# A spectral kernel of two heads: small column repairs given to another engine, the first loads put into one queue, a hint for the last branch, and a new order of the steps

## The chip, the core and the metric

The kernel runs on one core of a Trainium2 chip. Its engines are TensorE (PE, whose weight loads the profile lists apart as PEld), VectorE (DVE), ScalarE (ACT), GpSimd (POOL) and SyncE (SP). Each runs its own instructions in order; semaphores tie them together. SP issues nearly all loads, POOL the stores and a few small loads. The metric is the device time of one execution in microseconds, the median of several runs.

## What is computed

Two independent heads, joined along the last axis. Head A is a global filter: a real 2-D Fourier transform of a 2048 x 512 array, a product with a complex filter, and the transform back. Head B is Fourier mixing with the DFT matrices given as inputs.

```python
X = rfft2(A_x)                       # 1 x 2048 x 257, complex
a = irfft2(X * (A_w_r + 1j * A_w_i), s=(2048, 512))
h_re = einsum("bsd,ed->bse", B_x, dft_hid_re)
h_im = einsum("bsd,ed->bse", B_x, dft_hid_im)
b = einsum("ts,bse->bte", dft_seq_re, h_re) - einsum("ts,bse->bte", dft_seq_im, h_im)
return concatenate([a, b], axis=-1)
```

All data are float32. The two sequence matrices have 2048 x 2048 numbers each, 32 MB together.

## The kernel before, in words

The kernel does not multiply by the large matrices. It computes both heads by fast transforms, with tables of cosines and sines, and compares the given DFT matrices with those tables element by element. At the end one number, `flag`, says whether all compared equal. If they did not, a general path (`_b_from_c`, behind `tc.If` in L814) computes head B by plain products. With these inputs the general path is jumped over.

All work is cut into named steps, and `PLAN` (L23 to L39) is a list of their names. The loop at L808 runs through it and emits the instructions of each step, so the list sets the order in which PE, DVE, ACT and SP see them. POOL's instructions follow the same list. The steps:

- **Head A, forward.** `xa` loads a tile of x. `fold` (DVE, L344 to L353) adds and subtracts its mirrored halves. `hid` (PE, L360 to L365) transforms the hidden axis, `zs` (ACT, L369) copies the result from PSUM, `f16` (PE, L376) does a length-16 transform along the sequence, and `ys` (ACT, L380) scatters it into the large buffer `fz`. There are eight of `hid` to `ys` and five folds (0, 1, 3, 5, 7).
- **Head A, spectrum**, in eight slots n = 0 to 7 (slot 2 has a special form). `w` loads the filter and the table `fi`. `tr` (PE, L422) transposes, `ez` (ACT, L426) copies one half, `sf` (DVE, L432 to L434) combines mirrored halves, `fwd` (PE, L441) finishes the sequence transform, `prod` (DVE, L472 to L476) and `comb` (DVE, L480 to L484) multiply by the complex filter, `inv` (PE, L502) starts the way back, and `ev` (ACT, L509) writes into `fz`. In slot 2, `sx`, `g` and `spec` stand in for `sf`. Column 0 of the first half is an exception to the general formulas (two real spectra are packed into it). It is repaired by small operations of four numbers per partition: L434 in `sf`, L472 in `prod` (it puts a prepared filter column from `we` into `w`), and L484 in `comb` (a product with `sgn`).
- **Head A, inverse.** `hi` (PE, L537), `eu` (ACT, L542), `g16` (PE, L549), `sc` (ACT, L553), `eo` (DVE, L558) and the stores `st` (POOL) run eight times over the hidden axis and the length-16 transform. `hi` reads all of `fz`, so it starts after the last `ev`.
- **Head B.** `xb` loads, `xr` (ACT) reverses, `al` (PE, L629 and L630) and `av` (ACT) do the first transform in 16 pieces; `bh` (PE, L651 to L655), `hv` (ACT), `ro` (PE, L667), `y1` and `y3` (ACT), `y2` (DVE, L682) and the stores `pt` (POOL) do the rest in eight.
- **The comparison.** `cl` loads 1 MB of the given matrices, `cc` (DVE, L724) compares it with the table that `tt` loaded. There are 34 such pairs. `sg` (ACT) changes the sign of half a table in place. `rs`, `pf` and `flag` reduce the result.

`blk` is a ring of six buffers that the x tiles of both heads and the blocks of the comparison share; a load waits until the step that read the buffer's earlier content is done. The tiles named `pa` (three, two banks each) and `pb` (two, one bank each) are PSUM.

At the start ACT issues the first table `ta` (L298), SP the x tiles, and POOL the tile `eye`, the corner values `wsp`, `odd` and `turn`. Nine dummy products (L311) keep PE busy. `late` reloads `ta` with the tables of the inverse stage.

Of the kernel before, what the change touches and what calls it, by code (L numbers as in the profile page):

```python
# [24 lines left out]
ys0 xb2 fold5 f16_1 zs2 xb3 f16_2 ys1 xb1 hid3 ys2 cl3 cc1 hid4 zs3 fold7 cl4 f16_3 zs4 f16_4 ys3 hid5 ys4 cl5
cl6 cc2 hid6 zs5 w0 f16_5 zs6 cl7 xr0 hid7 ys5 w1 cc3 al0 zs7 f16_6 av0 cc4 sg0 f16_7 ys6 w2 cc5 al1 ys7 late
al2 av1 cc6 tr0 av2 tr1 ez0 tr2 sf0 ez1 al3 sf1 fwd0 xb4 av3 cc7 xb7 ez2 xb6 xb5 fwd1 xb8 cl8 prod0 sg1 tr3
xb9 xb10 comb0 fwd2 cl9 xb11 xb12 prod1 xb13 xr1 xb14 g2 al4 comb1 ez3 inv0 av4 cl10 sx2 al5 w3 ev0 al6 sf3
av5 spec2 al7 cc8 av6 w4 inv1 av7 xr2 prod2 tr4 xb15 ev1 al8 ez4 cc9 al9 av8 cl11 al10 av9 sf4 w5 al11 av10
comb2 fwd3 av11 cl12 cl14 xr3 cl13 fwd4 cc10 spy al12 al13 prod3 av12 al14 av13 al15 cc11 av14 w6 inv2 cl15  # L30
av15 cl16 cc12 tt2 cl17 comb3 bh8 cl19 ev2 bh0 hv8 prod4 inv3 hv0 comb4 tr5 w7 ev3 tr6 ez5 cc13 ro0 ez6 cc14
inv4 y10 bh1 ev4 y20 cl18 cl20 sf5 y30 rx sf6 tr7 hv1 ry bh2 cc15 ez7 pt0 ro1 hv2 cc16 tt3 fwd5 y11 cl21 ro2
y21 cl23 sg2 fwd6 sf7 y12 y31 y22 bh3 pt1 prod5 y32 fwd7 hv3 pt2 comb5 bh4 prod6 ro3 hv4 inv5 y13 comb6 ro4
ev5 y23 inv6 y14 prod7 y33 bh5 pt3 ev6 y24 comb7 y34 bh6 hv5 pt4 ro5 hv6 cc17 inv7 y15 bh7 ev7 y25 cl22 tt4
cc18 y35 ro6 hv7 pt5 hi0 y16 cc19 cc20 cl24 cl25 hi1 eu0 cc21 cl26 g16_0 y26 eu1 cl27 cc22 sg3 hi2 sc0 y36
cc23 pt6 hi3 eo0 eu2 cl28 cl29 cc24 g16_1 cc25 cl32 ro7 eu3 cc26 cl30 g16_2 y17 sc1 sg4 hi4 eo1 cl31 sc2 y27
st0 eo2 y37 pt7 hi5 cc27 eu4 cc28 cl33 g16_3 cc29 hi6 sc3 eu5 cc30 g16_4 eo3 cc31 g16_5 st1 eu6 sc4 hi7 sc5
eo4 eo5 cc32 st2 g16_6 eu7 cc33 g16_7 sc6 sc7 eo6 eo7 st30 rs st31 pf flag
# [893 lines left out]
```

## Time and profile before

| | |
|---|---|
| median of 3 runs | 192.7 us (192.49 to 192.76) |
| the profiled execution | 192.64 us, of which 190.3 us are the span from the first to the last instruction |
| moved by DMA | 66.05 MB, 346 GB/s over the span |
| granted TensorE clock | 0.983 |
| q1 (loads issued by SP) | 56.33 MB, 75.3% of the 16 DMA engines |
| q0 (POOL's stores and loads) | 9.08 MB, 12.3% |

The page's second part cuts the span into 40 slices of 4.76 us and gives the busy share of each in tenths. DVE and ACT read so:

```profile
DVE  1499999579899999999999999999999989779940
ACT  2015768699524493523444252354325273322300
```

A row of the groups reads: line, engine, operation, written tile <- read tiles, shape, count | busy us in all, mean ns of one | idle time of the engine just before these instructions, and what ended it. The costliest are the comparison and the first product of the inverse stage:

```profile
L724 DVE SCALAR_TENSOR_TENSOR blk<-blk,odd,tt 128x2048 f32<-128x2048 f32 x16 | 37.3, 2348 | 0.6 <-DMA blk<-in_cm 0.3
L537 PE MATMUL pa<-ta,fz 128*128 128x256 f32 x128 | 29.6, 388 | 0.0
```

A float32 product appears as more than one record, so counts of PE rows are twice those of the program. The view of one line lists operations as count: shortest/median/longest in ns, first and last start in us; a "q" behind an engine's name is its sequencer. In the view of waits a row names who waited for whom, the total in us, how often, and the longest.

### The profile page before, as it was taken

The page shows a single profiled execution, that of the slowest core. Times are in us where ns is not written, and L with a number is a line of the kernel's source. Part 1 is how long each engine was busy: PE and PEld are TensorE (multiplying, and loading weights), DVE is VectorE, ACT ScalarE, POOL GpSimd, SP SyncE. Part 2 cuts the span into 40 slices and gives each one's busy share as a digit, 9 for nine tenths or more (in the row PEclk, how much of TensorE's full clock was granted, in tenths as well). Part 3 has the DMA queues.
Part 4 walks back from the last instruction along what each step waited for, and adds up shares of the span by engine and source line. Part 5 has one row for each costly group of instructions (what it writes and reads, how often), then busy time and mean ns, then how long its engine had stood idle before and what let it go on. Part 6 is the DMA issues. An engine that isn't in the chain of part 4 may idle for free.

```text
span 190.3 us, 2768 instructions
## 1 busy us (share of the span) xinstructions
PE 169.9 (89%) x1017; PEld 147.1 (77%) x1017; DVE 166.3 (87%) x240; ACT 83.9 (44%) x114; POOL 23.6 (12%) x33
## 2 busy tenths in 40 slices
...
DVE  1499999579899999999999999999999989779940
ACT  2015768699524493523444252354325273322300
...
DMA  6979999999999999999999989234889999996551
GB/s 188 416 310 432 418 436 398 419 413 416 409 403 418 412 406 326 400 418 309 366 416 409 410 307 418 101 115 124 308 357 419 424 414 420 421 412 230 223 173 63
DMA packets 19619, 66.05 MB, mean 347 GB/s; under 512 B 1776, under 2 KB 2672, under 8 KB 18704
## 3 DMA queue, kind: packets, MB, share of 16 engines
q1 hardware_dynamic: 16784, 56.33, 75.3%
q0 software_dynamic: 2672, 9.08, 12.3%
q10 hardware_dynamic: 144, 0.39, 0.7%
q8 instruction: 10, 0.16, 0.3%
...
HBM read 57.41 MB, written 8.39 MB: 346 GB/s over the span
## 4 chain that ended last, share of the span: by engine, by line
DVE 52%; DMA 35%; issue 7%; SPq 1%; POOL 1%; DVEq 0%; POOLq 0%
DMA blk<-in_cm 27%; DVE blk L724 24%; DVE work L476 7%; DMA tt<-tab_hs 5%; DMA wsp_sb<-in_wsp 3%; DVE work L558 3%; DVE work L482 2%; DVE work L480 2%; DVE work L483 2%; DVE work L481 2%; DVE yb L682 2%; DVE work L433 2%; DVE work L432 2%; DVE work L344 1%; DVE work L682 1%
## 5 line engine op out<-in xcount | busy, mean ns | idle before, releaser
L724 DVE SCALAR_TENSOR_TENSOR blk<-blk,tt 128x2048 f32<-128x2048 f32 (+2 forms) x24 | 41.4, 1755 | 5.8 <-DMA blk<-in_cm 5.8
L724 DVE SCALAR_TENSOR_TENSOR blk<-blk,odd,tt 128x2048 f32<-128x2048 f32 x16 | 37.3, 2348 | 0.6 <-DMA blk<-in_cm 0.3
L537 PE MATMUL pa<-ta,fz 128*128 128x256 f32 x128 | 29.6, 388 | 0.0
L537 PEld LDWEIGHTS pa<-ta,fz 128*128 128x128 f32 x128 | 28.8, 305 | 0.4 <-issue 0.2
L542 ACT COPY work<-pa 128x1024 f32<-128x1024 f32 x8 | 8.1, 1014 | 20.7 <-PE pa L537 12.5
L476 DVE TENSOR_TENSOR work<-pa,w 128x1024 f32<-128x1024 f32 x14 | 16.5, 1220 | 0.6
L502 PEld LDWEIGHTS pa<-fi,work 128*128 128x128 f32 x112 | 13.4, 192 | 4.5 <-DVE work L484 2.6
L549 PEld LDWEIGHTS pa<-ta,work 128*128 128x128 f32 x128 | 15.3, 192 | 1.8 <-PE pa L549 1.2
L549 PE MATMUL pa<-ta,work 128*128 128x128 f32 x128 | 15.5, 275 | 1.0 <-DVE work L558 1.0
L380 ACT COPY fz<-pa 128x1024 f32<-128x1024 f32 x8 | 15.3, 1976 | 2.4 <-PE pa L376 2.4
L502 PE MATMUL pa<-fi,work 128*128 128x128 f32 x112 | 13.8, 276 | 2.4 <-DVE work L484 1.8
L376 PE MATMUL pa<-ta,work 128*128 128x128 f32 x128 | 15.1, 275 | 0.0
L369 ACT COPY work<-pa 128x1024 f32<-128x1024 f32 x8 | 8.1, 1013 | 15.8 <-PE pa L365 15.7
L376 PEld LDWEIGHTS pa<-ta,work 128*128 128x128 f32 x128 | 14.7, 192 | 0.0
L629 PE MATMUL pb<-fb,blk 128*128 128x200 f32 (+1 forms) x64 | 14.6, 309 | 0.0
L630 PE MATMUL pb<-fb,xr 128*128 128x200 f32 (+1 forms) x64 | 14.6, 309 | 0.0
L441 PE MATMUL pa<-work,fi 128*128 128x512 f32 x28 | 13.1, 595 | 1.4 <-DMA fi<-tab_fi 1.4
L509 ACT COPY fz<-pa 128x1024 f32<-128x1024 f32 x8 | 8.1, 1013 | 11.0 <-PE pa L502 7.9
L629 PEld LDWEIGHTS pb<-fb,blk 128*128 128x128 f32 x64 | 10.8, 190 | 0.5 <-issue 0.5
L558 DVE TENSOR_TENSOR work<-pa,work 128x512 f32<-128x512 f32 x16 | 10.1, 683 | 0.8 <-ACT work L553 0.8
L630 PEld LDWEIGHTS pb<-fb,xr 128*128 128x128 f32 x64 | 10.8, 190 | 0.0
L441 PEld LDWEIGHTS pa<-work,fi 128*128 128x128 f32 x28 | 5.1, 190 | 7.1 <-issue 6.8
...
## 6 DMA issues: line engine op xcount, KB each, us to landing
blk<-in_cm SPq DMA_DIRECT2D x32, 1024.0 KB, 12.3
...
```

The costliest lines, as they stand in the source:

```text
L369: act.copy(zs, flat(at["pd", i]))
L376: mm(y[:, r, c], zs[:, r, 128 * c : 128 * c + 128], f16, start=True, stop=True)
L380: act.copy(fz.rearrange("p c k (n g) -> p g (c k n)", g=16)[:, i::8], flat(at["py", i]))
L441: mm(flat(px[:, h]), ft[:, 0], flat(t[:, h]), start=True, stop=True)
L476: TT(out=m[:, h].rearrange("p i (r q) f -> p i r (q f)", r=2), in0=x2, in1=w2, op=MUL)
L502: mm(pi[:, i, q], lhs[i], it[:, 0], start=True, stop=True)
L537: mm(pu[:, k, h], gz[:, 2 * h + q, 2 * j + k], at["di"][:, h, q], start=q == 0, stop=q == 1)
L549: mm(po[:, k, q // 2, q % 2], u[:, k, q], at["g16"], start=True, stop=True)
L558: TT(out=ob[:, r, :, 2 * half : 2 * half + 2].rearrange("p k j s -> p j k s"), in0=at["po", j][:, :, 0], in1=sc, op=op)
L629: mm(bank[:, lo : lo + w], x[:, g, k], fb[:, n // 15, 0, :w], start=True, stop=False)
L630: mm(bank[:, lo : lo + w], xr[:, g, k], fb[:, n // 15, 1, :w], start=False, stop=True)
L724: dve.scalar_tensor_tensor(raw, raw, k, v, op0=MUL, op1=ALU.not_equal, accum_out=stat[:, i : i + 1])
```

## The change

- The repairs of column 0 leave DVE. L434 becomes the step `tf`, L472 the step `wf`, L484 the step `yf`, all on ACT; `yf` is a copy and a multiplication by -1 in place of one product with `sgn`, which goes away.
- The first table's 641 hidden-axis columns are loaded by SP, as the step `ta` behind `xa0`. The length-16 table moves into a tile `square` beside `eye`, loaded by POOL. `late` now loads 1024 columns into `ta` and, in a second load, the table of `g16` over the first half of `square`.
- `we` comes after `fold1`. There are 14 dummy products where there were 9.
- Twelve steps before the end, a branch hint is placed on PE, ACT and DVE for the branch over the general path, with a barrier for the step order that makes no engine wait.
- `PLAN` is a new list.

```diff
-xa0 xa1 xa2 xa3 tt0 cl0 xa5 xa7 we fb fold0 cl1 fold1 tt1 hid0 bt fold3 cl2 hid1 zs0 f16_0 zs1 cc0 xb0 hid2
+xa0 ta tt0 xa1 xa2 xa3 xa5 cl0 fb fold0 cl1 hid0 bt xa7 fold1 tt1 we hid1 zs0 cl2 fold3 f16_0 zs1 f16_1 ys0
...
-    tf = const("ta", 1152)[:, :769]
-    act.dma_start(tf, tabs["first"][:, :769])
-    eye = const("eye", P, src=tabs["first"][:, 769:], by=pool)
+    tf = const("ta", 1024)[:, :641]
+    square = const("square", 2, P, src=tabs["first"][:, 641:].rearrange("p (i f) -> p i f", i=2), by=pool)
+    f16, eye = square[:, 0], square[:, 1]
+    @step("ta")
+    def _():
+        load(tf, tabs["first"][:, :641])
...
-    for _ in range(9):
+    for _ in range(14):
...
-                dve.tensor_copy(t[:, 0, :, :, 0], pz[:, :, 0, :, 0])
+            @step(f"tf{n}")
+            def _():
+                act.copy(t[:, 0, :, :, 0], at["pz", n][:, :, 0, :, 0])
...
+        @step(f"wf{n}")
+        def _():
+            act.copy(at["w", n][:, 0, :, :, 0], we[:, e].rearrange("p f r -> p r f"))
...
-            dve.tensor_copy(w[:, 0, :, :, 0], we[:, e].rearrange("p f r -> p r f"))
...
-            TT(out=yo[:, 0, :, :, 0], in0=y[:, 0, :, :, 0], in1=sgn, op=MUL)
+        @step(f"yf{n}")
+        def _():
+            act.copy(yo[:, 0, 0, :, 0], y[:, 0, 0, :, 0])
+            act.mul(yo[:, 0, 1, :, 0], y[:, 0, 1, :, 0], -1.0)
...
-        tl = const("ta", 1152, src=tabs["late"], by=pool)
-        at["g16"] = tl[:, 1024:]
+        tl = const("ta", 1024, src=tabs["late"][:, :1024], by=pool)
+        pool.dma_start(f16, tabs["late"][:, 1024:])
...
-    for name in PLAN.split():
+    plan = PLAN.split()
+    for at_step, name in enumerate(plan):
+        if at_step == len(plan) - 12:
+            tc.no_sync_barrier()
+            tc.mark_branch_hint_location("general", hint="LikelyTaken", engines=[e.engine for e in (pe, act, dve)])
         steps.pop(name)()
...
-    with tc.If(small == 0):
+    with tc.If(small == 0, label="general"):
```

The list moves steps in many places; three of them matter below. The first is on DVE, where the spectral stage begins. Before the change, the rows of `sf0`, `sf1`, `cc7`, `prod0` and `comb0` (`pa` is PSUM, `blk` a block of the comparison, `work` the working buffer):

```order
L432 TENSOR_TENSOR work<-pa,work 128x2x256
L433 TENSOR_TENSOR work<-work,pa 128x2x256
L434 COPY work<-pa 128x4
L432 TENSOR_TENSOR work<-pa,work 128x2x256
L433 TENSOR_TENSOR work<-work,pa 128x2x256
L434 COPY work<-pa 128x4
L724 SCALAR_TENSOR_TENSOR blk,stat<-blk,tt 128x2048
L472 COPY w<-we 128x4
L476 TENSOR_TENSOR work<-pa,w 128x1024 x2
```

DVE's rows of the change at the same place (lines are 3 to 13 higher there):

```order
L435 TENSOR_TENSOR work<-pa,work 128x2x256
L436 TENSOR_TENSOR work<-work,pa 128x2x256
L435 TENSOR_TENSOR work<-pa,work 128x2x256
L436 TENSOR_TENSOR work<-work,pa 128x2x256
L485 TENSOR_TENSOR work<-pa,w 128x1024 x2
L489 TENSOR_TENSOR work<-work 128x2x2x128
L490 TENSOR_TENSOR work<-work 128x2x256
L491 TENSOR_TENSOR work<-work 128x2x256
L492 TENSOR_TENSOR work<-work 128x2x256
L737 SCALAR_TENSOR_TENSOR blk,stat<-blk,tt 128x2048
```

The small copies are gone, and the comparison `cc7` has moved from ahead of `prod0` to behind `comb0`.

The second place is ACT's, at the same point of the change: `ez0`, `wf0`, `ez1`, `av2`, `tf0`, `wf1`, `av3`, `tf1`, `wf2`, `ez2` and `yf0` in this order (`yall` is head B's buffer):

```order
L429 COPY work<-pa 128x512
L477 COPY w<-we 128x4
L429 COPY work<-pa 128x512
L647 COPY yall<-pb 128x43x8
L440 COPY work<-pa 128x4
L477 COPY w<-we 128x4
L647 COPY yall<-pb 128x43x8
L440 COPY work<-pa 128x4
L477 COPY w<-we 128x4
L429 COPY work<-pa 128x1024
L496 COPY work<-work 128x2
L497 ACTIVATE work<-work 128x2
```

The rows of L440, L477, L496 and L497 are new on this engine; each stands in line with copies that wait for PE.

The third place is the end on DVE. Before, the last two comparisons, the last two `eo` (four rows) and the reduction:

```order
L724 SCALAR_TENSOR_TENSOR blk,stat<-blk,odd,tt 128x2048
L724 SCALAR_TENSOR_TENSOR blk,stat<-blk,tt 128x2048
L558 TENSOR_TENSOR work<-pa,work 128x2x2x128 x4
L798 TENSOR_REDUCE rs<-stat 128x1
L806 TENSOR_SCALAR flag<-pb 128x1
```

The same place of the change on DVE, with the hint:

```order
L737 SCALAR_TENSOR_TENSOR blk,stat<-blk,odd,tt 128x2048
L942 BRANCH_PREFETCH_HINT
L571 TENSOR_TENSOR work<-pa,work 128x2x2x128 x4
L737 SCALAR_TENSOR_TENSOR blk,stat<-blk,tt 128x2048
L811 TENSOR_REDUCE rs<-stat 128x1
L819 TENSOR_SCALAR flag<-pb 128x1
```

The last comparison has moved behind the last `eo`, so the last stores can leave before it.

More of the change, by code (lines that the diff above doesn't have):

```diff
@@ L23 @@
 PLAN = """
-xa0 xa1 xa2 xa3 tt0 cl0 xa5 xa7 we fb fold0 cl1 fold1 tt1 hid0 bt fold3 cl2 hid1 zs0 f16_0 zs1 cc0 xb0 hid2
[L25 to L38, printed above, removed]
+xa0 ta tt0 xa1 xa2 xa3 xa5 cl0 fb fold0 cl1 hid0 bt xa7 fold1 tt1 we hid1 zs0 cl2 fold3 f16_0 zs1 f16_1 ys0
@@ new lines @@
+fold5 xb0 xb3 xb2 hid3 ys1 hid2 zs3 cc0 cl3 f16_3 zs2 cc1 cl4 f16_2 ys3 hid5 ys2 xb1 fold7 hid4 zs5 cl5 f16_5
+zs4 cl6 cc2 hid6 ys5 w0 xb4 f16_4 hid7 cc3 ys4 zs6 zs7 f16_6 w1 cc4 xr0 f16_7 sg0 w2 cc5 al0 ys6 late ys7 al1
+av0 tr0 cc6 av1 tr1 ez0 wf0 al2 ez1 sf0 al3 av2 sf1 tf0 wf1 fwd0 cl7 av3 xb7 tf1 xb6 xb5 tr2 prod0 xb8 wf2
+xb10 fwd1 ez2 cl9 cl8 comb0 fwd2 xb11 cc7 yf0 xb9 xb12 inv0 g2 xr1 prod1 w3 sg1 al4 ev0 sx2 al5 w4 av4 tr3
+comb1 av5 spec2 al6 ez3 al7 av6 sf3 yf1 tr4 cl11 av7 prod2 xr2 cl12 inv1 xb13 ez4 tf3 al8 xb15 wf3 comb2 ev1
@@ new lines @@
+al9 av8 xb14 wf4 fwd3 av9 sf4 yf2 spy cc8 al10 w5 tf4 al11 av10 cc9 tr5 av11 cl10 inv2 ez5 prod3 cl14 xr3 cl13
+wf5 comb3 al12 w6 ev2 al13 av12 al14 cc10 av13 yf3 al15 av14 fwd4 sf5 cl15 av15 cc11 tf5 bh8 prod4 tt2 tr6 hv8
+cl16 wf6 inv3 ez6 comb4 bh0 w7 ev3 sf6 fwd5 yf4 hv0 cc12 tf6 ro0 cc13 cl18 tr7 wf7 cl17 y10 fwd6 ez7 y20 prod5
+y30 rx bh1 ry cc14 pt0 bh2 hv1 ro1 comb5 hv2 cl21 cl19 inv4 y11 y21 bh3 yf5 ev4 sf7 y31 prod6 ro2 tf7 pt1 hv3
+fwd7 y12 y22 bh4 comb6 y32 pt2 inv5 hv4 cc15 yf6 ro3 ev5 inv6 cc16 y13 cl20 tt3 bh5 ev6 y23 cl22 sg2 prod7 ro4
```

14 lines of the change are left out of this document (8 added, 6 removed).

## The prediction

> **What bounds the kernel now.** I read the page's busy shares first, then the span cut at places where the program changes its character, then what stands at each cut.
>
> ```profile
> PE 169.9 (89%) x1017; PEld 147.1 (77%) x1017; DVE 166.3 (87%) x240; ACT 83.9 (44%) x114; POOL 23.6 (12%) x33
> DMA  6979999999999999999999989234889999996551
> 0.00:48.80 48.80, 43.78 (x308) 39.58 (x309) 37.58 (x51) 28.50 (x25) 3.19 (x11) 1.00 0.96 386
> 48.80:129.30 80.50, 75.59 (x423) 59.53 (x422) 78.29 (x126) 35.48 (x63) 8.20 (x11) 1.00 0.92 354
> 129.30:134.70 5.40, 5.40 (x30) 4.08 (x29) 5.40 (x14) 2.92 (x5) 0.72 (x2) 1.00 0.48 143
> 134.70:180.30 45.60, 44.60 (x260) 43.63 (x258) 42.44 (x49) 16.40 (x22) 9.94 (x8) 1.00 0.92 370
> 183.40:190.30 6.90, 0.00 (x0) 0.00 (x0) 0.00 (x0) 0.00 (x0) 0.27 (x1) 0.53 0.43 144
> ```
>
> The windows give PE, PEld, DVE, ACT, POOL, clock, DMA share and GB/s. No engine is bound everywhere. Up to 48.8 us (the last comparison before the first `sf`) the DMA share is 0.96 and DVE has 11 us idle: the loads decide. From 48.8 to 129.3 (the end of `comb7`) DVE works 78.29 of 80.50 us and PE 75.59: both are nearly full, DVE a little more. From 134.7 (the first `hi`) to 180.3 (the last `g16`) PE is at 44.60 of 45.60. After 183.4 nothing computes. So the edits have to be priced in four stages.
>
> **Front: the first table, `fold0` ahead of `we`, 14 warm matmuls: 0.** DVE waits for the tiny load `wsp` while x is already there, and later waits for blocks of `cm`:
>
> ```profile
> 7.51 0.19 DVE L389 TENSOR_TENSOR we<-wsp_sb 128x16 f32<-128x16 f32 x1 [6.09 <-DMA wsp_sb<-in_wsp]
> 7.78 0.69 DVE L344 TENSOR_TENSOR work<-blk 128x512 f32<-128x512 f32 x1
> 13.30 20.61 DMA blk<-in_cm
> 36.32 15.76 DMA blk<-in_cm
> DVE blk L724 <- DMA blk<-in_cm: 6.1, 5, 2.6
> ta<-tab_late POOLq DMA_DIRECT2D x1, 576.0 KB, 7.0
> ```
>
> `fold0` can start up to 2.6 us earlier (an estimate: about 5.2 instead of 7.78). But the chain runs through transfers until 52 us, and the set of loads issued ahead of `cl6` is the same in both programs (`ta`, six x loads, `tt0`, `tt1`, `fb`, `bt`, four `xb`, `cl0` to `cl5`); only their order differs. DVE will idle at `xa1`, which now queues behind `ta` and `tt0`, and at `xa7`, now behind `bt`, and reach `cc6` at about the same time. I take 0, between -2.6 (all of it passes) and +1.5 (the `late` table, which now waits for the last `hid` and no longer for the last `f16`, takes its 576 KB before `cl6`, at the 386 GB/s of this window 1.5 us). The longer warm-up hides in PE's idle time ahead of the first `hid`.
>
> **Spectral stage: the repairs.** The three small DVE operations are seen with their neighbours:
>
> ```profile
> 49.42 0.68 DVE L433 TENSOR_TENSOR work<-work,pa 128x512 f32<-128x512 f32 x1
> 50.13 0.17 DVE L434 COPY work<-pa 128x4 f32<-128x4 f32 x1
> 50.21 0.68 DVE L432 TENSOR_TENSOR work<-pa,work 128x512 f32<-128x512 f32 x1
> 58.93 0.68 DVE L483 TENSOR_TENSOR work<-work 128x512 f32<-128x512 f32 x1
> 59.72 0.17 DVE L484 TENSOR_TENSOR work<-work,sgn 128x4 f32<-128x4 f32 x1
> 59.80 0.17 DVE L472 COPY w<-we 128x4 f32<-128x4 f32 x1
> 60.06 1.23 DVE L476 TENSOR_TENSOR work<-pa,w 128x1024 f32<-128x1024 f32 x1
> L484 DVE TENSOR_TENSOR work<-work,sgn 128x4 f32<-128x4 f32 x8 | 1.3, 167 | 0.3
> L472 DVE COPY w<-we 128x4 f32<-128x4 f32 x8 | 1.3, 166 | 0.0
> L434 DVE COPY work<-pa 128x4 f32<-128x4 f32 x7 | 1.2, 165 | 0.2
> ```
>
> An operation starts 0.08 us before its neighbour's end when nothing ties the two. So without L434 the next would start at 50.02 instead of 50.21: 0.19 each. Without L484 and L472 together L476 would start at 59.53 instead of 60.06: 0.53 for the pair. That is 7 x 0.19 + 8 x 0.53 = **5.6 us** off DVE's path; where L484's gap is shorter it is less, so I use 5.2.
>
> They go to ACT, whose like operations are these:
>
> ```profile
> 66.56 0.17 ACT L463 COPY work<-pa 128x4 f32<-128x4 f32 x1 [0.32 <-DVE cn L458]
> 80.16 0.18 ACT L492 COPY work<-cn 1x2 f32<-1x2 f32 x1
> 80.28 0.20 ACT L493 ACTIVATE work<-cn 1x2 f32<-1x2 f32 x1
> 122.49 0.17 DVE L484 TENSOR_TENSOR work<-work,sgn 128x4 f32<-128x4 f32 x1
> 122.71 1.86 PEld L502 LDWEIGHTS pa<-fi,work 128*128 128x128 f32 x16 [2.58 <-DVE work L484]
> ```
>
> 7 `tf` and 8 `wf` of 0.17 and 8 `yf` of 0.38 add 5.7 us to an engine that is busy 35.48 of 80.50: its total is no bound. What is added is a hand-over: PE's `fwd` and `inv` wait for DVE, then ACT. Here PE started 0.05 us after L484; with ACT between I put 0.4 us, more if ACT is inside a copy. `wf` stands slots ahead of its `prod` and is hidden. One place loses its cover: before, `cc7` (2.3 us) stood between `sf1` and `prod0`; now `prod0` follows `sf1` at once, and `tf0` and `fwd0` have to fit into one `sf` of 1.2 us:
>
> ```profile
> L441 PE MATMUL pa<-work,fi 128*128 128x512 f32 x28 | 13.1, 595 | 1.4 <-DMA fi<-tab_fi 1.4
> ```
>
> 13.1 / 7 = 1.9 us for a `fwd`, so DVE idles there about 1.9 + 0.4 - 1.2 = 1.1 us. DVE's own sum to the end of `comb7` is 80.5 - 5.2 - 0.4 (the wait for `cc7`) + 1.1 = 76.0; then `yf7`, `inv7` and `ev7` (0.4 + 2.0 + 1.2) would allow `hi0` at 128.4. **PE decides instead**: from 48.8 to 134.7 it was busy 75.59 + 5.40 = 81.0 of 85.9 us, and its work ahead of `hi0` stays the same but for `ro7` (0.7, now ahead). With no idle time at all `hi0` could start at 48.8 + 81.7 = 130.5. Of the 4.9 us of idle I leave 1.5 (at `fwd0`, which waits for `tf0`, and at `inv1`, which waits for `yf1` behind ACT's queue): `hi0` at 132.0, **-2.7 us**. Bounds: -4.2, and 0 if every new hand-over costs PE what DVE gains.
>
> **Inverse stage: 0.** Eight `hi` and eight `g16` take 8 x 3.45 + 8 x 1.87 = 42.6 us by these rows:
>
> ```profile
> 173.63 3.24 PE L537 MATMUL pa<-ta,fz 128*128 128x256 f32 x14
> 176.71 3.73 PE L549 MATMUL pa<-ta,work 128*128 128x128 f32 x32
> ```
>
> (3.24 for 14 lacks two records; 16 come to some 3.45.) Before, the stage took 45.6 with `ro7` in it: 2.3 idle. The new order runs `hi` up to three ahead, and I let half of the idle go: -1.1 - 0.7 for `ro7`. Against that, `cc33` now follows the last `eo`: from the last `g16` to the flag there are `sc7` and `eo7` (2.0), `cc33` (2.2) and the reduction with the flag (0.8), 5.0 against 3.1 before: +1.9. Sum about 0; bounds -1.1 and +1.9.
>
> **Tail.** After the flag every engine loads it and jumps over the general path:
>
> ```profile
> 183.20 0.16 DVE L806 TENSOR_SCALAR flag<-pb 128x1 int32<-128x1 f32 x1 [0.47 <-PE pb L802]
> L814 PEldq COMPARE_BRANCH  x1: 4264/4264/4264, 184.5 to 184.5; - x1
> L814 ACTq EVENT_SEMAPHORE  x1: 17/17/17, 189.2 to 189.2; - x1
> L814 SPq EVENT_SEMAPHORE  x8: 17/17/17, 185.3 to 185.8; - x8
> SPq L925 <- DMA out_a<-work: 1.8, 1, 1.8
> L925 POOLq DRAIN  x3: 51/109/4188, 184.7 to 190.1; - x3
> L925 SPq DRAIN  x3: 7/7/13, 189.4 to 189.8; - x3
> L925 SPq EVENT_SEMAPHORE  x14: 17/28/1796, 185.9 to 190.3; - x14
> ```
>
> PE's jump takes 4.26 us; ACT's is short, but its next instruction comes only at 189.2. SP waits for nothing but 1.8 us of the last store and then for those engines; POOL's drain lasts 4.19. If the hint has the target ready, SP goes through without a stop: last of its eight at 185.8, the 1.8 us store wait gone because the last store now leaves 2.2 us of comparison earlier, ten more steps of 0.06 us, and from SP's first drain to the end 0.9 as now (189.4 to 190.3): 185.8 + 0.7 + 0.1 + 0.9, an end near 187.5, **-2.8 us**. Bounds: 0, and -2.8.
>
> In the Trainium skill, "Runtime: NRT & Kernel Launch", section "Instruction fetch mechanics", a taken branch whose target lies outside the two loaded blocks forces a fetch before execution goes on; the 4.26 us agree. The same section calls prefetch purely sequential. By that a hint could load nothing out of order, the tail would stay at 6.9 and the sum would be 189.9; no run here shows it yet.
>
> **Sum.** The profiled execution took 192.64 (span 190.3 and 2.34 around it), the median shown is 192.7. 192.64 + 0 - 2.7 + 0 - 2.8 = **187.1 us**.
>
> **Rivals.**
> - *The tail stays.* The hint loads nothing, or POOL's 4.19 us drain is its own and not the store's: the branch at 184.5 plus 4.2 and the barrier give -0.5 at most. Then 192.64 - 2.7 and between 0 and 0.5: 189.4 to 189.9. For it: POOL gets no hint, and its drain ends with the fetches. Against: the drain also ends 1.1 us after SP's store wait does. 0.20.
> - *Everything passes.* PE loses all 4.9 us of idle and the inverse stage its 1.1: 192.64 - 4.2 - 1.1 - 2.8 = 184.5. 0.13.
> - *The repairs bring nothing.* PE's stalls move elsewhere, the tail alone counts: 192.64 - 2.8 = 189.8. 0.05.
> - *Slower: ACT's queue.* `tf` and `yf` put 15 in-order ACT operations between DVE and PE. If each holds PE for c us, the loss is 15c. Against a gain of 5.5 that decides from c = 0.37; with c = 0.6, a 0.6 us copy ahead in half of the cases, 192.64 - 5.5 + 9.0 = 196.1. For it: PE is nearly full, so its waits are not made up. Against: `al` and `bh` products stand on PE around most of these places. 0.12.
>
> **Numbers.** The forecast has 0.50. The range 183.2 to 191.3 holds it, the first three rivals and their scatter, and leaves out the slower one. A difference under 0.2% can't be told from no change. Faster by more than that: 0.84; within: 0.04 (the second rival with a lost front); slower: 0.12.
>
> **What would show it.** Right: `cc6` ends at 48 to 50 us; DVE idle about 1 us before `prod0`; `hi0` near 132; a short PE branch and an end some 4.2 us behind the flag. Wrong: a branch of 4 us again; PE idle charged to ACT's small `work` copies in many places; `cc6` after 51; DVE waiting for `cm` after 150.

## The result, and the profile after

| | before | changed |
|---|---|---|
| median | 192.66 us (192.49 to 192.89, 6 runs) | 191.34 us (190.94 to 191.75, 6 runs) |
| ratio | | 0.9931, 95% interval 0.9914 to 0.9947 |
| profiled execution | 192.64 us, span 190.3 | 191.75 us, span 190.0 |

The change gains 0.7%, where 2.9% were forecast, and the time lies 0.04 us outside the range. The stages of the changed kernel, from the view of windows (from : to, length, busy time of PE, PEld, DVE, ACT, POOL with the number of records, clock, DMA share, GB/s):

```profile
0.00:51.35 51.35, 45.16 (x309) 39.88 (x310) 37.68 (x51) 28.32 (x25) 3.59 (x10) 0.97 0.97 377
51.35:129.10 77.75, 77.32 (x431) 60.72 (x429) 74.65 (x104) 40.44 (x94) 10.09 (x11) 1.00 0.93 341
129.10:134.20 5.10, 5.10 (x29) 3.83 (x28) 5.10 (x11) 2.98 (x6) 2.28 (x3) 1.00 1.02 383
134.20:179.20 45.00, 43.66 (x257) 42.85 (x255) 40.82 (x47) 15.93 (x21) 5.94 (x7) 1.00 0.91 366
184.30:190.00 5.70, 0.00 (x0) 0.00 (x0) 0.00 (x1) 0.00 (x0) 0.00 (x0) 0.50 0.12 37
```

The front (to the end of `cc6`) is 51.35 us long instead of 48.80. The spectral stage is shorter, 77.75 instead of 80.50, and PE is busy 77.32 of it. The tail is 5.7 instead of 6.9.

The forecast cut the program where DVE ends `cc6`. Two other marks turned out to carry more: the first transpose `tr0`, with which PE begins the spectrum, and the first `hi`. Their rows, of before and of the changed kernel, in the view of one line (shortest/median/longest in ns, first and last start):

```profile
L422 PE MATMUL pa<-eye,fz x64: 272/273/328, 46.8 to 103.3; 128*128 128x128 f32 x64
L537 PE MATMUL pa<-ta,fz x128: 378/384/482, 135.1 to 176.5; 128*128 128x256 f32 x128
...
L425 PE MATMUL pa<-square,fz x64: 270/273/328, 48.5 to 99.7; 128*128 128x128 f32 x64
L550 PE MATMUL pa<-ta,fz x128: 379/384/559, 134.2 to 174.7; 128*128 128x256 f32 x128
```

And the windows between these marks, before and changed:

```profile
46.80:135.10 88.30, 83.39 (x470) 65.90 (x469) 86.09 (x139) 39.99 (x71) 9.21 (x13) 1.00 0.90 343
...
48.50:134.20 85.70, 85.25 (x479) 67.38 (x480) 82.02 (x114) 45.28 (x104) 12.37 (x13) 1.00 0.94 345
```

By the first products the stretch went from 88.35 to 85.65 us, and PE in it from 4.9 us of idle time to 0.45. It also holds more work: PE is busy 85.25 us instead of 83.39, as one piece of `al` and `ro7` have come into it (112 and 22 records instead of 104 and 20). But it starts 1.7 us later, so that `hi0` comes only 1.0 sooner. All of the difference, in the profiled executions: front +1.7, `tr0` to `hi0` -2.7, `hi0` to the flag +1.9 (48.2 to 50.1), tail -1.3, what lies around the span -0.5; sum -0.9, the difference of 192.64 and 191.75. (The changed kernel's profile is of the slowest of its six executions; the medians differ by 1.3.)

What DVE and SP waited for in the changed kernel (view of waits: total, times, longest):

```profile
DVE blk L737 <- DMA blk<-in_cm: 9.3, 5, 4.2
DVE work L347 <- DMA blk<-in_xa: 7.0, 3, 3.4
DVE work L485 <- PE pa L447: 1.1, 1, 1.1
SPq L942 <- DVEq L831: 2.1, 1, 2.1
```

The 1.1 us ahead of `prod0` is the stall that was forecast. The wait of 3.4 is `fold1` for `xa1`, and the longest for a block, 4.2 us, lies in the last stage at 160 us.

The tail, by the branch's line and the closing line:

```profile
L831 PEldq COMPARE_BRANCH  x1: 480/480/480, 184.9 to 184.9; - x1
L831 DVEq COMPARE_BRANCH  x1: 84/84/84, 185.0 to 185.0; - x1
L831 ACTq EVENT_SEMAPHORE  x1: 17/17/17, 185.3 to 185.3; - x1
L831 DVEq EVENT_SEMAPHORE  x1: 21/21/21, 189.0 to 189.0; - x1
...
L942 POOLq DRAIN  x3: 45/97/2409, 185.4 to 189.7; - x3
```

PE's branch is short now and ACT goes on at 185.3. DVE's branch is short too, but its next instruction comes 4.0 us later, and SP waits 2.1 us for it.

### The profile page after: what moved, and what is told of

It reads as the page before. It is cut to its first block, busy times and chain, and to the rows that moved or that the text cites. A ratio compares the mean times of both kernels' runs of the same rounds, so it can differ in the third digit from the quotient of the medians.

```text
span 190.0 us, 2792 instructions
## 1 busy us (share of the span) xinstructions
PE 171.7 (90%) x1022; PEld 147.6 (78%) x1022; DVE 162.8 (86%) x217; ACT 88.3 (46%) x145; POOL 23.4 (12%) x32
## 4 chain that ended last, share of the span: by engine, by line
DMA 35%; PE 30%; DVE 25%; issue 4%; ACT 1%; SPq 1%; DVEq 0%
DMA blk<-in_cm 16%; DVE blk L737 15%; DMA blk<-in_xa 14%; PE pa L515 5%; DMA w<-in_wa 4%; PE pa L447 4%; PE pb L643 4%; PE pb L642 4%; DVE work L571 3%; PE pb L668 3%; PE pa L518 2%; PE pa L425 2%; PE pa L451 2%; PE pb L680 2%; PE pb L664 1%
## 5 line engine op out<-in xcount | busy, mean ns | idle before, releaser
L383 ACT COPY fz<-pa 128x1024 f32<-128x1024 f32 x8 | 15.2, 1976 | 4.3 <-PE pa L379 4.3
L347 DVE TENSOR_TENSOR work<-blk 128x1024 f32<-128x1024 f32 (+1 forms) x10 | 10.1, 1009 | 7.0 <-DMA blk<-in_xa 7.0
L379 PE MATMUL pa<-square,work 128*128 128x128 f32 x128 | 15.3, 276 | 0.7 <-ACT work L372 0.7
L372 ACT COPY work<-pa 128x1024 f32<-128x1024 f32 x8 | 8.0, 1019 | 16.5 <-PE pa L368 16.5
L379 PEld LDWEIGHTS pa<-square,work 128*128 128x128 f32 x128 | 14.9, 194 | 0.9 <-ACT work L372 0.9
L562 PEld LDWEIGHTS pa<-square,work 128*128 128x128 f32 x128 | 14.8, 192 | 0.7 <-issue 0.6
L562 PE MATMUL pa<-square,work 128*128 128x128 f32 x128 | 15.0, 276 | 0.3 <-DVE work L571 0.3
L367 PE MATMUL pa<-ta,work 128*128 128x256 f32 x32 | 10.6, 417 | 0.0
```

Source lines behind the costliest of these rows:

```text
L347: TT(out=us[:, h, own].rearrange("p c k f -> p c (k f)"), in0=xs(b)[:, own, 0], in1=xs(b)[:, own, 1], op=op)
L367: mm(even, v[:, 0, 1, r], hd0, start=True, stop=False)
L379: mm(y[:, r, c], zs[:, r, 128 * c : 128 * c + 128], f16, start=True, stop=True)
L383: act.copy(fz.rearrange("p c k (n g) -> p g (c k n)", g=16)[:, i::8], flat(at["py", i]))
L562: mm(po[:, k, q // 2, q % 2], u[:, k, q], f16, start=True, stop=True)
```

## The experiments

Where two kernels are compared, both were timed in five rounds against the kernel before; "us" are medians. Marks within the span are from the profiled executions.

### The hint

`n1_no_hint`: the changed kernel without the hint.

```diff
-        if at_step == len(plan) - 12:
-            tc.no_sync_barrier()
-            tc.mark_branch_hint_location("general", hint="LikelyTaken", engines=[e.engine for e in (pe, act, dve)])
```

> The changed kernel with the branch hints taken out, all else kept. Theory (the hint works on PE and ACT but not on DVE, so it is worth only part of the forecast): the PE branch lasts about 4.3 us again in place of 0.48, the flag stays near 184.3, the end comes 6.5 to 7 us behind it, and the time is 1.3 us above the changed kernel, about 192.6. Rival (the hint is worth the forecast 2.8 us and the rest of the change loses): about 194.1. Second rival (DVE's late restart was the bound before as well, the hint is worth nothing): 191.3, as the changed kernel.

191.26 us, ratio 0.9925 (0.9913 to 0.9938): as the changed kernel. The second rival holds, that the hint is worth nothing.

```profile
L828 PEldq COMPARE_BRANCH  x1: 3739/3739/3739, 184.5 to 184.5; - x1
L828 ACTq EVENT_SEMAPHORE  x1: 17/17/17, 184.9 to 184.9; - x1
L828 DVEq EVENT_SEMAPHORE  x1: 21/21/21, 188.3 to 188.3; - x1
```

PE's branch is long again, but it ends when DVE starts anyway. And ACT goes on after 0.4 us without any hint: its quick start isn't the hint's doing.

`n5_before_hint`: the kernel before with the same three lines added.

> The kernel before with the branch hints for PE, ACT and DVE alone, twelve steps ahead of the end. Theory (the hint seldom brings in the block behind the branch; the changed kernel without it took the same time): at least PE or DVE still starts again 3.5 to 4.7 us behind its branch, and the time is within 0.4 us of the kernel before, 192.3 to 193.1. Rival (the hint works where no other load of code comes between it and the branch, as in the forecast): all three start within 0.6 us, 189.9 to 191.5.

192.61 us, ratio 0.9994 (0.9984 to 1.0004): no change, as the theory said.

```profile
L818 PEldq COMPARE_BRANCH  x1: 490/490/490, 184.9 to 184.9; - x1
L818 DVEq EVENT_SEMAPHORE  x1: 21/21/21, 189.9 to 189.9; - x1
L818 ACTq EVENT_SEMAPHORE  x1: 17/17/17, 189.9 to 189.9; - x1
```

Here ACT has its hint and is as late as DVE, 5 us. The hint helped PE alone.

`n2_dve_hint_later`: DVE's hint behind `eo7`.

```diff
+        if at_step == len(plan) - 6:
+            tc.no_sync_barrier()
+            tc.mark_branch_hint_location("general", hint="LikelyTaken", engines=[dve.engine])
```

> The changed kernel with DVE's hint six steps later, behind eo7, ahead of cc33; PE and ACT keep theirs. Theory (between the old place of the hint and the branch DVE went over into its next block of code, so that what the hint had fetched was replaced): DVE's first instruction behind its branch comes within 0.6 us of it instead of 4.0, the wait of SP for DVE (2.1 us) goes, and POOL's drain, which ended at 187.80, is late next: 1.0 to 1.2 us off, about 190.2. Rival (DVE's wait has another cause than the place of the hint): DVE's 4.0 us stay, 191.3.

191.57 us, ratio 0.9936 (0.9922 to 0.9949); DVE goes on 4.1 us behind its branch. The theory falls: the place of DVE's hint is not the reason.

### Where DVE's branch stands in its code

ACT started at once in the changed kernel with and without the hint, and late in the kernel before. What differs is its number of instructions, 33 more. `n4` (below), which has the new order and the hint but not these 33, has ACT late again, 4.1 us behind its branch. A load of 8 KB of code stands at 176 us in the changed kernel, when ACT is a few instructions ahead of its branch. So DVE was lengthened.

`n10_dve_pads`: 36 writes behind the first memsets and a step `pads` with 38 behind `fold0`.

```diff
+    pad = const("pad", 1)
+    for _ in range(36):
+        dve.memset(pad[0:1], 0.0)
```

> The changed kernel with 74 small writes to an unused tile on DVE, 36 while it waits for xa0 and 38 while it waits for xa1, so that DVE's branch comes some 14 instructions behind the start of its next block of code instead of 60 ahead of it. Theory (an engine starts again at once behind the branch if its stream went into a new block shortly before it, so that the next block, with the branch's target, is loaded already: ACT did in every run with its 33 more instructions, hint or not, and in neither run without them): DVE's first instruction behind the branch comes within 0.6 us of it, an 8 KB load of code stands at about 180 us, and the tail falls to 4.2 to 4.6 us where PE is quick as well, else to about 5.1; the time is 0.3 to 1.2 us less, 190.1 to 191.0. Rival (DVE's late start is no matter of its place in the code): 4 us again, 191.3.

189.86 us, ratio 0.9874 (0.9836 to 0.9911), 1.5 us below the changed kernel. In the DMA queues, the stretch from 168.5 to 170 us now holds a load of code that the changed kernel doesn't have there:

```profile
q14 instruction: 1, 0.01, 1.3%
...
L839 PEldq COMPARE_BRANCH  x1: 484/484/484, 183.4 to 183.4; - x1
L839 DVEq EVENT_SEMAPHORE  x1: 21/21/21, 184.0 to 184.0; - x1
```

DVE goes on 0.6 us behind its branch. POOL's drain (2.41 us from 183.8) is now what ends last, and flag to end takes 4.3 us. In all seven profiles with the longer DVE stream (n10, n12 to n17) DVE was quick, in none of the twelve without it. The Trainium skill, "Runtime: NRT & Kernel Launch", section "Instruction fetch mechanics", says that a taken branch stalls if its target is outside the loaded window; these runs agree, with 4.0 us against 0.6.

`n13_pads_no_hint`: n10 without the hint.

> n10_dve_pads without the branch hints. Theory (the hint acts on PE alone, now and then, and this shows once DVE no longer holds the end): PE's jump 3.5 to 4.3 us in every run, DVE 0.6, tail 4.9 to 5.4, and the time 0.3 to 1 us above n10's 189.86, with less spread. Rival (the hint does nothing): as n10, 189.9 with the same spread. Second rival (the quick start of DVE came from its hint after all): DVE 4 us again and 191.3.

190.16 us, ratio 0.9854 (0.9839 to 0.9869). DVE 0.6 us, PE 3.6, flag to end 5.3. The profile is as the theory has it: DVE's quick start isn't the hint's, PE's is. In time the two kernels can't be told apart, since their intervals overlap.

`n14_pe_hints`: n12 (below) with three hints, for PE alone.

```diff
+        if at_step in (len(plan) - 12, len(plan) - 8, len(plan) - 4):
+            tc.no_sync_barrier()
+            tc.mark_branch_hint_location("general", hint="LikelyTaken", engines=[pe.engine])
```

> n12_late_pads with the hint given to PE alone, twelve, eight and four steps ahead of the end, and none to ACT and DVE. Theory (each hint on PE is taken or dropped by chance of the moment, so three of them are seldom all dropped; those of ACT and DVE never did anything): PE's jump 0.5 us, a 16 KB load of code between 173 and 181 us, tail 4.3, DVE and ACT still quick, time 0.2 to 0.5 us below n12. Rival (the hints of the other engines mattered, or PE's outcome is set by something else than the try): PE's jump 3.5 us or more, or DVE or ACT late, time as n12 or above.

189.86 us, ratio 0.9846 (0.9815 to 0.9876). PE's branch took 3.3 us and no code was loaded for it. More tries did not help in this one profile, and the time is no lower than n12's. Of fifteen profiles with a hint on PE, five have the short branch, each with a 16 KB load of code 1.2 to 2.2 us behind the hint; what decides stays open.

### Who shortened the spectral stage

`n4_repairs_dve`: the changed kernel and order with `tf`, `wf` and `yf` as DVE operations.

```diff
-                act.copy(t[:, 0, :, :, 0], at["pz", n][:, :, 0, :, 0])
+                dve.tensor_copy(t[:, 0, :, :, 0], at["pz", n][:, :, 0, :, 0])
...
-            act.copy(yo[:, 0, 0, :, 0], y[:, 0, 0, :, 0])
-            act.mul(yo[:, 0, 1, :, 0], y[:, 0, 1, :, 0], -1.0)
+            TT(out=yo[:, 0, :, :, 0], in0=y[:, 0, :, :, 0], in1=sgn, op=MUL)
```

> The changed kernel and order with the three kinds of repairs (tf, wf, yf) done by DVE again, as one copy, one copy and one multiply for each slot. Theory (the repairs are what shortened the spectral stage): cc6 as in the changed kernel, comb7 at about 132 to 134 instead of 129.1, and as the last stage is held by loads only part comes through: 1.5 to 3 us more, 192.8 to 194.3. Rival (the new order shortened the stage): comb7 within 1 us of 129.1 and the time within 0.4 us of 191.3. Second rival (the stage is longer, the last stage gives it all back, since its loads come when they come): comb7 at 132 or later, but the time still near 191.3.

192.16 us, ratio 0.9967 (0.9955 to 0.9979), 0.8 us above the changed kernel. `comb7` ends at 131.5 instead of 129.1: the stage is 2.4 us later, and a third of that is left in the time, less than the theory had and more than its second rival.

`n11_before_act`: the kernel before with the repairs on ACT, each step right behind the one it mends, no hint.

> The kernel before, in its own order and without hints, with the repairs alone moved to ACT (each step put right behind the one whose data it mends). Theory (the repairs are what shortens the spectral stage, and the new order only costs, in the front and by cl30): cc6 as before (48.9), comb7 at 126 to 127 instead of 129.2, and 1 to 2.5 us of it come through, so 190.2 to 191.7, at or below the changed kernel. ACT, with 33 more instructions, starts again quickly behind its branch. Rival (in the old order ACT's small copies come late and hand DVE's saved time back as waits, which the new order avoids): comb7 within 0.8 us of 129.2 and the time within 0.4 us of 192.7.

191.41 us, ratio 0.9934 (0.9918 to 0.9950): the same as the whole change. `comb7` ends at 127.8 instead of 129.2, 1.4 us sooner. The windows from `tr0` to `hi0` of n4, then of n11:

```profile
47.60:135.80 88.20, 85.62 (x479) 67.19 (x480) 83.41 (x137) 41.10 (x73) 12.44 (x13) 1.00 0.91 339
...
46.70:135.10 88.40, 84.22 (x471) 65.93 (x470) 83.71 (x116) 43.11 (x102) 10.21 (x13) 1.00 0.90 346
```

Both are as long as before the change (88.3), but not for the same reason. The repairs alone (n11) leave PE 4.2 us of its 4.9 us of idle time. The order alone (n4) leaves 2.6, but has brought the extra `al` and `ro7` into the stretch. Only the two together fill PE (0.45) and make the stretch shorter. n11 gains at another place. Its `hi0` stands where it stood, but from `hi0` to the flag it takes 47.1 us instead of 48.2, most likely since DVE comes to its remaining comparisons sooner.

### The front

`n3_late_later`: SP loads the late tables behind `w7` (at 93 and 94 us) instead of POOL at 41 and 45.

```diff
-        tl = const("ta", 1024, src=tabs["late"][:, :1024], by=pool)
+        tl = const("ta", 1024, src=tabs["late"][:, :1024], by=sync)
...
-        pool.dma_start(f16, tabs["late"][:, 1024:])
+        load(f16, tabs["late"][:, 1024:])
```

> The changed kernel with the 576 KB of the late tables issued by SP behind w7, at about 105 us, into the stretch of 107 to 124 us in which the DMA moved little, instead of by POOL at 41 and 45 us. Theory (their packets between those of cl5, cl6, w0 and w1 made the front longer): the block of cc6 lands 1.5 to 2.6 us earlier than 49.05 and cc6 ends at 49 to 50 instead of 51.35; as the last stage is held by its loads, 0.8 to 2 us of it come through, 189.4 to 190.6. Rival (the front is longer by the loads ahead, xa1 behind the table tt0 and xa7 behind bt, and the sum of bytes decides anyway): cc6 still ends at 51 to 51.5 and the time stays within 0.3 us of 191.3.

190.26 us, ratio 0.9883 (0.9860 to 0.9905), 1.1 us below the changed kernel. DVE's timeline around `cc6` (start, length; in brackets the idle time before it and what ended it), first of the changed kernel, then of n3:

```profile
49.08 2.35 DVE L737 SCALAR_TENSOR_TENSOR blk<-blk,odd,tt 128x2048 f32<-128x2048 f32 x1 [1.53 <-DMA blk<-in_cm]
51.35 0.69 DVE L435 TENSOR_TENSOR work<-pa,work 128x512 f32<-128x512 f32 x1
...
47.52 2.35 DVE L737 SCALAR_TENSOR_TENSOR blk<-blk,odd,tt 128x2048 f32<-128x2048 f32 x1 [0.20 <-DMA blk<-in_cm]
50.15 0.69 DVE L435 TENSOR_TENSOR work<-pa,work 128x512 f32<-128x512 f32 x1 [0.27 <-ACT work L429]
```

`sf0`, the first operation of the spectrum (L435), stands behind `cc6` on DVE. Without the late tables in the way `cc6` ends 1.56 us sooner, and `sf0` then waits for ACT. From `tr0` to `hi0` it takes 84.8 us instead of 85.7:

```profile
48.30:133.10 84.80, 84.74 (x479) 67.34 (x480) 81.10 (x114) 44.79 (x104) 12.38 (x13) 1.00 0.94 350
```

PE has no idle time left there.

`n8_xa_first`: n3 with the x tiles ahead.

```diff
-xa0 ta tt0 xa1 xa2 xa3 xa5 cl0 fb fold0 cl1 hid0 bt xa7 fold1 tt1 we
+xa0 ta xa1 xa2 xa3 tt0 cl0 xa5 xa7 fb fold0 cl1 hid0 bt fold1 tt1 we
```

> As n3_late_later, with xa1, xa2 and xa3 ahead of the table tt0 and xa7 behind xa5, as in the kernel before (the first table stays behind xa0 in SP's queue). Theory (by the end of the front it is bound by the sum of bytes ahead of the block of cc6, which is the same): DVE's wait at xa1 falls from 3.4 to about 1 us, but cc6 ends within 0.3 us of 49.87 and the time is within 0.4 us of 190.3. Rival (the late xa1 and xa7 are what is left of the longer front): cc6 ends at about 48.9 and the time is 0.8 to 1 us less, 189.4.

190.92 us, ratio 0.9917 (0.9893 to 0.9941). The last fold ends 1.0 us sooner (33.71), `cc6` at 50.03, but `tr0` stays (48.49 against 48.35): no gain. The reason stands in ACT's timeline of the changed kernel, where `ys` (L383) writes `fz`, `zs` is L372, `xr` L631 and L632, `sg` L754:

```profile
38.47 1.95 ACT L383 COPY fz<-pa 128x1024 f32<-128x1024 f32 x1 [1.99 <-PE pa L379]
40.21 1.97 ACT L372 COPY work<-pa 128x1024 f32<-128x1024 f32 x2
42.67 0.20 ACT L631 COPY xr<-blk 128x4 f32<-128x4 f32 x1 [0.49 <-issue]
42.77 1.04 ACT L632 COPY xr<-blk 128x1020 f32<-128x1020 f32 x1
43.72 1.15 ACT L754 ACTIVATE tt<-tt 128x1024 f32<-128x1024 f32 x1
44.77 3.70 ACT L383 COPY fz<-pa 128x1024 f32<-128x1024 f32 x2
```

`xr0` needs `xb1`, which the new order loads behind `cl4`; it lands at 42.60 in the trace, and the copy starts 0.07 us later. Behind it stand `sg0`, which no comparison needs before `cc8`, and only then the last two `ys`. `tr0` waits for them.

`n12_late_pads`: n3 and n10 together.

> n3_late_later and n10_dve_pads together (late tables behind w7, 74 small writes on DVE so that its branch stands behind the start of a block of code). Theory (the two act at different places, 1.1 us in the front and 1.4 in the tail): about 188.8 us, tail 4.3 where PE's jump is short and about 5.1 where it is long, so times spread by some 0.8 us. Rival (the writes in the front cost what the late tables gave, since fold1 ends later): about 189.9.

189.43 us, ratio 0.9827 (0.9797 to 0.9857): a little of both gains. The 38 writes between `fold0` and `fold1` took 0.11 us each and put the last fold to 35.65, as the rival feared. The gains also overlap: in n10 the writes had already delayed the late tables (issued at 42.3 us instead of 40.9), and `cc6` ended at 49.0 there instead of 51.4, with `sf0` waiting for ACT. So little of n3's gain was left to take.

`n15_act_front`: n12 with ACT's queue cleared.

```diff
-... xb0 xb3 xb2 hid3 ... ys2 xb1 fold7 ... hid6 ys5 w0 ... cc4 xr0 f16_7 sg0 w2 cc5 al0 ys6 ys7 al1
+... xb0 xb3 xb2 xb1 hid3 ... ys2 fold7 ... hid6 ys5 xr0 w0 ... cc4 f16_7 w2 cc5 al0 ys6 ys7 sg0 al1
```

> n12_late_pads with xb1 loaded right behind xb2, the copy xr0 between ys5 and ys4 and the sign change sg0 behind ys7, so that nothing that waits stands ahead of ys6 and ys7 on ACT. Theory (in the front DVE waits for blocks of cm, and ACT's copies have slack of under 0.5 us against them): ys7 ends 1 to 2 us sooner than in n12, the first transposes with it, but comb7 and the time move by less than 0.4 us. Rival (ACT's last two copies into fz set the start of the spectral stage): comb7 and the time 1 to 1.7 us less.

189.51 us, ratio 0.9835 (0.9799 to 0.9870). In the profile `tr0` is 1.5 us sooner than in n12 and `hi0` 1.6, for the rival; the medians don't show it. PE's branch at the end was long in n15's profile (3.4 us) and short in n12's (0.48), which hides 0.9 us of it there. Not settled by this run alone.

`n16_front_free`: n15 with 44 writes ahead of `fold0` and 24 ahead of `cc3`, none between the folds.

> n15_act_front with the small writes on DVE put where it waits anyway: 44 ahead of fold0, 24 ahead of cc3, none between fold0 and fold1. Theory (now that the late tables are gone, the start of the spectral stage is set by ACT's copies into fz behind the last fold): ys7 ends at about 47 us instead of 48.6, comb7 at 127 to 127.6 instead of 128.3, and the time is 188.5 to 189.1. Rival (blocks of cm set it, cc6 keeps its 49.1): comb7 within 0.4 us of 128.3 and the time within 0.4 us of 189.5. DVE's start behind the branch stays quick (0.6 us) in both.

188.35 us, ratio 0.9762 (0.9723 to 0.9801): 1.2 us below n15 (the two intervals just touch), `comb7` at 127.28, and `cc6` at 49.05 as there. The marks behave as expected: ACT's copies set the start, not the blocks of `cm`.

`n17_xa_front`: n16 with the loads of n8.

> n16_front_free with xa1 to xa3 ahead of tt0 and xa7 behind xa5, as in n8. Theory (PE is full from tr0 on, so the end follows tr0, and tr0 follows the last fold once ACT's queue no longer holds it): the last fold ends about 1 us sooner (33.7 to 34), tr0 starts at 46.5 to 47 instead of 47.64, the first hi 84.7 us behind it, at 131.2 to 131.8 instead of 132.35, and the time is 0.5 to 1 us below n16's 188.35. Rival (the loads of cm hold DVE and so the end, or the blocks that now land later for xa7 cost as much): the first hi within 0.3 us of 132.35 and the time within 0.4 us of 188.35.

187.05 us, ratio 0.9693 (0.9672 to 0.9714). The edit that gave nothing in n8 gives 1.3 us here. ACT's timeline (L640 `xr`, L386 `ys`, L762 `sg`) and the window from `tr0` to `hi0`:

```profile
36.88 1.04 ACT L640 COPY xr<-blk 128x1020 f32<-128x1020 f32 x1
37.82 1.88 ACT L386 COPY fz<-pa 128x1024 f32<-128x1024 f32 x1
39.50 1.97 ACT L375 COPY work<-pa 128x1024 f32<-128x1024 f32 x2
42.70 3.79 ACT L386 COPY fz<-pa 128x1024 f32<-128x1024 f32 x2 [1.23 <-PE pa L382]
46.23 1.23 ACT L762 ACTIVATE tt<-tt 128x1024 f32<-128x1024 f32 x1
...
46.60:131.30 84.70, 84.67 (x480) 67.30 (x479) 81.80 (x114) 45.91 (x105) 12.38 (x13) 1.00 0.94 354
```

The marks of these kernels side by side, in us:

| | last fold ends | `tr0` | `hi0` | `tr0` to `hi0` | flag |
|---|---|---|---|---|---|
| before | 33.62 | 46.80 | 135.15 | 88.35 | 183.36 |
| changed | 34.74 | 48.52 | 134.17 | 85.65 | 184.30 |
| n4 (repairs on DVE) | 34.39 | 47.62 | 135.77 | 88.15 | 184.43 |
| n11 (before, repairs on ACT) | 33.55 | 46.74 | 135.07 | 88.33 | 182.16 |
| n3 (late tables later) | 34.67 | 48.35 | 133.09 | 84.74 | 182.22 |
| n8 | 33.71 | 48.49 | 133.27 | 84.78 | 182.68 |
| n12 | 35.65 | 50.22 | 135.01 | 84.79 | 183.24 |
| n16 | 34.92 | 47.64 | 132.35 | 84.71 | 180.86 |
| n17 | 33.60 | 46.62 | 131.32 | 84.70 | 179.81 |

In these five kernels with the late tables away, `hi0` follows `tr0` by 84.7 to 84.8 us, whenever `tr0` is; in n9 and n7 (below) it was 85.28 and 85.55. Marks of single profiles also scatter: up to `tr0`, PE, DVE, ACT and SP have the same instructions in n4 as in the changed kernel, and its `tr0` is 0.9 us sooner.

### The last stage

`n6_cc33_before_eo7`:

```diff
-g16_7 sc6 eo6 sc7 eo7 st30 cc33 st31 rs pf flag
+g16_7 sc6 eo6 sc7 cc33 eo7 st30 st31 rs pf flag
```

> The changed kernel with the last comparison cc33 ahead of eo7 instead of behind it, nothing else. Theory (DVE is busy without a pause there, so the order sets no flag; but the two last stores of out_a are issued 2.3 us nearer the flag, and the reading of the flag and the loads of code behind the branch then stand behind their packets, which is what the tail of 6.98 us in the kernel before showed): flag within 0.3 us of the changed kernel's as measured from comb7, tail (flag to end) 6.5 to 7.0 instead of 5.4 to 5.8, so about 192.3. Rival (the stores have nothing to do with it): tail 5.4 to 5.8 and 191.3.

191.35 us, ratio 0.9950 (0.9930 to 0.9970): no change in time, as the rival said. But the theory was right about the tail, 6.74 us, with the last store in it again. SP's waits in n6, then DVE's branch and SP's wait for DVE in the kernel before:

```profile
SPq L942 <- DMA out_a<-work: 1.8, 1, 1.8
SPq L942 <- DVEq L831: 1.4, 1, 1.4
...
L814 DVEq COMPARE_BRANCH  x1: 72/72/72, 184.6 to 184.6; - x1
L814 DVEq EVENT_SEMAPHORE  x1: 21/21/21, 189.2 to 189.2; - x1
SPq L925 <- DVEq L814: 1.1, 1, 1.1
```

In both, SP has to wait for DVE once more after it has the store, so its 1.8 us for the store are not what makes the tail long. What is later is the code behind the branch. In the kernel before and in n6, n5 and n11, the first load of code starts 1.8 to 1.9 us behind DVE's branch, as the last packets of the store end (at 186.6 us before), and DVE goes on after 4.6 to 5.1 us. In every other kernel the last store is done sooner: the load starts 0.9 to 1.0 us behind the branch, and DVE, where it is late, goes on after 3.8 to 4.3.

The flag of n6 came 1.8 us sooner than the changed kernel's, not at the same place, which makes up for its tail. DVE's own work from `comb7` to the flag is the same in both; its waits differ (4.8 against 3.1 us in sum), and in n1 they were 4.1. Nearly all of the difference is in waits for blocks of `cm` between 156 and 166 us, ahead of `cc33`. So how much of the 1.8 us is scatter, and whether the place of `cc33` costs anything ahead of the flag, isn't shown.

`n7_cc15_early`: n3 with `cc15`, `cl20` and `tt3` behind `comb5`.

```diff
-inv4 y11 y21 bh3 ... hv4 cc15 yf6 ro3 ev5 inv6 cc16 y13 cl20 tt3 bh5
+inv4 y11 cc15 cl20 tt3 y21 bh3 ... hv4 cc16 yf6 ro3 ev5 inv6 y13 bh5
```

> As n3_late_later, with cc15 behind comb5 instead of behind comb6, cl20 and tt3 right behind it, and cc16 where cc15 was: SP, which waits for these blocks, issues cl20 and what is queued behind it some 8 us sooner, into the stretch in which the DMA moves little. Theory (the last stage is DVE's, less its waits for blocks of cm): the waits of 2.4 and 0.6 us at 157 and 165 us go to below 1 in sum, and the time falls 1.5 to 2.5 us below n3_late_later's 190.3. Rival (the two comparisons put ahead of the spectral work make comb7 as much later as the loads come sooner, or DMA isn't what is waited for): within 0.5 us of 190.3, comb7 2 us later or the waits unchanged.

190.77 us, ratio 0.9910 (0.9891 to 0.9928). The rival: `comb7` 1.0 us later, the waits unchanged (2.3 and 0.6 us).

`n9_cl30_order`: n3 with `cl30` behind `cl29`.

```diff
-cl26 cl30 y27 cl27 ... eo1 cl31
+cl26 y27 cl27 ... eo1 cl30 cl31
```

> As n3_late_later, with the load cl30 behind cl29, in the order in which DVE uses the blocks, instead of ahead of cl27. Theory (in the last stage the blocks land one behind the other, and the 1 MB of cl30, which DVE uses only 13 us after it lands, stands ahead of cl27 to cl29, for each of which DVE then waits): the wait of 2.4 us at 157 us and that of 0.6 us at 165 us go to below 1 us in sum, and the time falls by 1 to 2 us from 190.3. Rival (the stores of out_b and out_a, bunched in that stretch, hold the blocks up, and their order sets nothing): the waits stay near 3 us in sum and the time within 0.4 us of 190.3.

190.13 us, ratio 0.9859 (0.9837 to 0.9881): as n3. DVE's longest wait in the last stage, of the changed kernel, n3 and n9:

```profile
160.31 2.35 DVE L737 SCALAR_TENSOR_TENSOR blk<-blk,odd,tt 128x2048 f32<-128x2048 f32 x1 [4.18 <-DMA blk<-in_cm]
...
157.41 2.35 DVE L737 SCALAR_TENSOR_TENSOR blk<-blk,odd,tt 128x2048 f32<-128x2048 f32 x1 [2.36 <-DMA blk<-in_cm]
...
171.03 2.35 DVE L737 SCALAR_TENSOR_TENSOR blk<-blk,odd,tt 128x2048 f32<-128x2048 f32 x1 [2.69 <-DMA blk<-in_cm]
```

In n9 the wait only moves, from 157 to 171 us. The order of the blocks sets where DVE waits and not how long. That the sum of bytes does is likely (DMA share 0.91 in that window) but wasn't shown.

## Why the prediction failed, point by point

- **Front, 0: wrong, and the largest single loss.** By the forecast's own mark, the end of `cc6`, it was +2.55 (48.80 to 51.35), against a bound of +1.5. By `tr0` it was +1.7, and the late tables held `sf0` for another 0.9 inside the next stretch. The price of the late tables was right, 1.5 us: `cc6` moved by 1.56 in n3. What failed is that I set them off against an earlier `fold0`. It did start at 4.63 us instead of 7.78, but `fold1` then waited 3.4 us for `xa1`, and the last fold ended 1.1 us later than before. And I took the end of `cc6` as the end of the front. With the late tables away, PE's stretch begins with `tr0`, behind ACT's last copies into `fz`. The diff moves `xb1` behind `cl4` on SP, and `xr0`, which needs it, stands ahead of these copies on ACT; I read DVE's waits and not ACT's queue. n15 to n17 show it: each us taken from `tr0` came through to `hi0`, while `cc6` stayed at 49.1.
- **Spectral stage, -2.7: the mechanism right, the exact number luck.** 88.35 to 85.65 from `tr0` to `hi0`, with the 1.1 us stall at `prod0` and PE as the bound. But two misses cancel in it: PE lost 4.5 us of idle time where 3.4 were forecast (0.45 left, not 1.5), and its work between these marks grew by 1.9 us, where 0.7 for `ro7` was forecast, by the `al` that came in. From the end of `cc6`, the forecast's own mark, to `hi0` the stage shrank by 3.5 us. The 5.2 us of DVE's path were not seen either: its busy time in that stage fell from 78.29 to 74.65, 3.6 us, and the runs don't separate what gaps between operations went with it. That did no harm, since PE decides. (ACT's added work is 15 x 0.17 + 8 x 0.38 = 5.6 us, not 5.7; nothing hangs on it.)
- **Inverse stage, 0: mis-sized.** +1.9 from `hi0` to the flag in the profile, the upper bound; +1.2 to +1.3 in n1 and n2, whose steps are the same. From the last `g16` to the flag it took 2.2 us more than before (5.1 instead of 2.9), where +1.9 was forecast for `cc33`. The gains set against it, 1.1 of PE's idle time and 0.7 for `ro7`, came as 0.3 in sum: `hi0` to the last `g16` took 45.0 instead of 45.3. The idle time wasn't there to be halved: the forecast worked out 2.3 us from a sum of rows, while its own window has PE busy for 44.60 of 45.60 us. In the changed kernel PE is idle for 1.3, and DVE waits up to 4.2 us for a block of `cm`.
- **Tail, -2.8: half of it, and not by the hint.** -1.3 came, in two parts. Some 0.5 us is ahead of the branch: each engine's load of the flag is shorter (SP's takes 0.49 us instead of 1.02, in n6 0.48); why, wasn't tested. 0.7 us is DVE going on 4.0 us behind its branch instead of 4.7, since the load of its code no longer starts behind the last store's packets: n6 brings that back. The wait of 1.8 us for the store, which the forecast took off, was covered by the wait for DVE. The hint's part did not come: PE got its code in this profile, but DVE, whose hint fetched nothing, holds the end. "If the hint has the target ready" is the step that failed (n1, n5). The rival *the tail stays* named this for its reason, though with a time 1.4 to 1.9 us too low, as the front was wrong in it too. The reckoning that gave 189.9 lets no hint load anything: PE's five loads behind a hint speak against it, while DVE's and ACT's hints loaded nothing where they were needed.
- **Slower by ACT's queue: no.** PE was idle for 0.45 us in the whole stage; no small copy of ACT held it there. ACT's queue did cost time, but in the front, by `xr0` and `sg0`.
- Of the signs of being wrong, two came: `cc6` ended after 51 us, and DVE waited for `cm` after 150. Of those of being right, the short branch of PE came without the short tail (5.7 us, not 4.2).
- The forecast of 187.1 and n17's 187.05 are alike by chance: n17's tail is 5.2 us, not 4.2, and its front is 0.2 us shorter than before.

n17 is faster than both kernels: 2.2% below the changed one (187.05 to 191.34, from separate sets of runs against the same kernel before).
